# Attention with pooled keys and a squared-ReLU feed-forward: the queries of chunks 2 to 11 are turned one step sooner, and their scores stay where they were

## The chip, the cores and the metric

One core of one Trainium2 chip runs the whole problem. The metric is the device time of the launch in microseconds (us). The core's engines run side by side, each with its own queue of instructions in the order of the program: TensorE (PE, matmuls), VectorE (DVE), ScalarE (ACT), GpSimd (POOL) and SyncE (SP), whose queue issues every DMA. An instruction at the head of a queue that waits holds up all that stand behind it in that queue.

## The reference

Each of 8 batches has 8 heads of 576 tokens with 64 numbers each. Keys and values are averaged over groups of 8 tokens, so each head has 72 pooled keys. A feed-forward net of 512 to 2048 to 512 follows, on the 4608 tokens of all batches.

```python
def _attn_ref(q, k, v):
    k_p = k.reshape(B, H, Sp, 8, D).mean(axis=3)
    v_p = v.reshape(B, H, Sp, 8, D).mean(axis=3)
    scores = (1.0 / np.sqrt(D)) * np.matmul(q, k_p.transpose(0, 1, 3, 2))
    scores = scores - np.max(scores, axis=-1, keepdims=True)
    attn = np.exp(scores)
    attn = attn / (np.sum(attn, axis=-1, keepdims=True) + 1e-09)
    return np.matmul(attn, v_p)

x = attn_out.transpose(0, 2, 1, 3).reshape(B * S, H * D)
h = np.maximum(x @ w_in, 0.0)
out = h * h @ w_out
```

## The kernel before

**Chunks and steps.** The 4608 tokens are cut into 12 chunks of 384. A chunk's feed-forward runs in 16 steps, one for each 128 columns of the hidden layer, so that the program is a row of 192 steps (and two at the end), numbered here `16 c + fc`. Step s emits for PE, in this order: the hidden matmuls of step s (`hidden`, tile `h`), then what attention work for PE is due in that step, then the output matmuls of step s-2 (`project`, tile `o`, LAG is 2). From chunk 1 on each factor is split in a high and a low part, so `hidden` has 12 matmuls and `project` 9. What follows for the other engines stands in this order: the split of step s-1's hidden values (`split_hidden`: ACT writes `gh`, DVE `gl`), then the second halves of the step's attention work on PE (`later`: the copies out of PSUM), then the rest of the attention work in the order in which it was registered, then ReLU (`activate`: ACT writes `r`; DVE squares it from chunk 2 on), and, in a chunk's last step of `project`, the copies of the three output banks by ACT (`store`, tile `ob`) and their DMAs.

**Attention of the next chunk.** While a chunk is in its feed-forward, the next one's attention is computed in four head pairs. Each goes through eight stages, each at a step of its own:

```python
    stages = (transpose_q, scores, exponents, send_sums, fetch_sums, reciprocals, fetch_reciprocals, weigh_values)
        for p in range(NPAIR):
            s = c * NFC + first[p]
            at(s - QL, load_q, c, p)
            for d, f in zip(offsets, stages):
                at(s + d, f, c, p)
```

`transpose_q` turns the queries on PE (four matmuls into the PSUM tile `qps`); its second half splits them into the one tile `st`: two ACT casts and two DVE subtractions. `scores` multiplies `st` with the keys `kl` and `kh` (`sps`), and ACT copies the scores to `sc`; POOL takes the maximum over the 72 keys (`mx`). `exponents` subtracts it (DVE), takes the exponential (ACT), and POOL sums it (`tot`). The sums go through DRAM (`rs`, `rc`), DVE takes reciprocals (`rr`), these go out and come back spread over the partitions (`rd`, `rb`). `weigh_values` multiplies with the pooled values `vp` on PE (`av`), DVE scales by `rb`, and ACT and DVE split the result into `xh` and `xl`, the input of the next chunk's `hidden`.

The steps are written out by hand in `STEADY` (chunks 2 to 11) and `EARLY` (chunk 1): the first tuple has the step at which each pair begins, relative to the chunk's first step, and the second the stages' distances from it. With a pair every four steps, several pairs are under way at a time.

**A chunk's layout.** A chunk of one batch alone (2, 3, 5, 6, 8, 9, 11) and a chunk over two batches (4, 7, 10) write `st` in different strides.

**Keys and values of a new batch** (`kv_steps`, from `KV0` = 31 steps before the chunk that needs them first, which are chunks 3, 4, 6, 7, 9 and 10): six loads of keys, each pooled two steps later on DVE (`kp`: a reduction and a copy), two turns of pooled keys on PE (`transpose_k`, tile `kps`) in the relative steps 5 and 8, each split by ACT and DVE into `kh` and `kl`, and eight pooled values on DVE (`vp`). The first turn needs the keys pooled in relative step 4.

**Buffers.** PSUM has three banks for attention (`ps_a`), two for `h`, and one for each of the three `o`. `st` has one buffer, `sc` two. In steps 14 to 29 the weights are split as well (`split_weights`: an ACT copy `w_i` or `w_o` and a DVE subtraction each).

Of the kernel before, what the change touches and what calls it, by code (L numbers as in the profile page):

```python
# [32 lines left out]
def pooled_attn_relu2_ffn(  # L33
# [43 lines left out]
    PRO, RATE, MARGIN = 5, 2, 1  # L77


    STEADY = ((-22, -18, -14, -10), (0, 1, 3, 4, 5, 6, 7, 8))  # L80
    KV0 = -31
    EARLY = ((-19, -16, -13, -10), (0, 2, 3, 5, 5, 6, 7, 8))

# [185 lines left out]
    def segments(c):  # L269
        t, segs = c * CH, []  # L270
        while t < (c + 1) * CH:
            b = t // S
            n = min((b + 1) * S, (c + 1) * CH) - t
            segs.append((b, t - c * CH, n))
            t += n
        return segs
# [361 lines left out]
    for c in range(1, NCH):  # L638
        first, offsets = EARLY if c == 1 else STEADY
        for b, _, _ in segments(c):  # L640
# [64 lines left out]
```

## Time and profile before

| | |
|---|---|
| median of 3 runs | 981.8 us (981.43 to 993.95) |
| the profiled execution | 978.9 us |
| its span, first to last instruction | 977.2 us |
| mean granted TensorE clock | 0.997 |
| PE busy | 947.3 us (97%) |
| DVE busy | 629.2 us (64%) |
| ACT busy | 425.8 us (44%) |
| POOL busy | 401.2 us (41%) |

The profile's "timeline" has one row for each run of like instructions: start in us, duration in us, engine, operation, output tile and inputs, shapes, the count, and in brackets how long the engine had been idle before and what ended it. SPq is the DMA queue on SP. "Waits" sums such idle times. "Windows" gives the busy time of each engine in a stretch. A pair of rows of a same kind may overlap a little, since an engine begins the next instruction before the last has drained; so the step lengths are better read from one start to the next.

### The profile page before, as it was taken

The page shows a single profiled execution, that of the slowest core. Times are in us where ns is not written, and L with a number is a line of the kernel's source. Part 1 is how long each engine was busy: PE and PEld are TensorE (multiplying, and loading weights), DVE is VectorE, ACT ScalarE, POOL GpSimd, SP SyncE. Part 2 cuts the span into 40 slices and gives each one's busy share as a digit, 9 for nine tenths or more (in the row PEclk, how much of TensorE's full clock was granted, in tenths as well). Part 3 has the DMA queues.
Part 4 walks back from the last instruction along what each step waited for, and adds up shares of the span by engine and source line. Part 5 has one row for each costly group of instructions (what it writes and reads, how often), then busy time and mean ns, then how long its engine had stood idle before and what let it go on. Part 6 is the DMA issues. An engine that isn't in the chain of part 4 may idle for free.

```text
span 977.2 us, 13363 instructions
## 1 busy us (share of the span) xinstructions
PE 947.3 (97%) x4888; PEld 785.9 (80%) x4888; DVE 629.2 (64%) x1034; ACT 425.8 (44%) x847; POOL 401.2 (41%) x209
## 2 busy tenths in 40 slices
PE   6889989999999999999999999999999999999998
PEld 5544458878888888888888888888888888888997
DVE  5869997886775555776776554777677455453221
ACT  2745457674334344334434434433443434432322
POOL 4398635463444434343435335343534434340000
PEclk9999999999999999999999999999999999999999
DMA  9944203112211002112112001211221100100000
GB/s 244 354 147 163 82 17 98 49 51 82 60 56 49 25 26 74 57 52 87 49 50 74 19 23 60 66 48 36 98 57 43 58 26 17 58 10 9 33 1 32
DMA packets 53361, 64.45 MB, mean 66 GB/s; under 512 B 14936, under 2 KB 34480, under 8 KB 53296
## 3 DMA queue, kind: packets, MB, share of 16 engines
q1 hardware_dynamic: 53296, 63.61, 20.9%
q8 instruction: 38, 0.62, 0.3%
q14 instruction: 27, 0.22, 0.1%
HBM read 53.87 MB, written 9.71 MB: 65 GB/s over the span
## 4 chain that ended last, share of the span: by engine, by line
PE 77%; DVE 13%; issue 5%; ACT 4%; POOL 0%; DMA 0%; POOLq 0%; DVEq 0%; ACTq 0%; SPq 0%
PE o L29 34%; PE h L29 33%; PE sps L29 3%; PE av L29 3%; DVE wf_o L29 3%; DVE wf_i L29 2%; PE qps L29 2%; DVE st L29 2%; DVE r L29 1%; ACT st L29 1%; DVE vp L29 1%; DVE sc L29 1%; ACT gh L29 1%; DVE rb L29 1%; ACT xh L29 1%
## 5 line engine op out<-in xcount | busy, mean ns | idle before, releaser
L29 PE MATMUL h<-xh,w_i 128*128 128x384 f32 x1408 | 389.0, 337 | 0.0
L29 PE MATMUL o<-w_o,gh 128*128 128x512 f32 x1056 | 333.7, 397 | 0.0
L29 POOL PARTITION_ALL_REDUCE tot<-sc x88 | 250.2, 2890 | 192.5 <-issue 179.3
L29 PEld LDWEIGHTS h<-xh,w_i 128*128 128x128 f32 x1408 | 258.7, 188 | 8.4 <-issue 0.5
L29 POOL PARTITION_ALL_REDUCE mx<-sc x88 | 138.2, 1618 | 268.8 <-ACT sc L29 268.8
L29 PE MATMUL h<-xl,w_i 128*128 128x384 f32 x704 | 237.9, 338 | 0.0
L29 PEld LDWEIGHTS o<-w_o,gh 128*128 128x128 f32 x1056 | 193.4, 189 | 32.8 <-issue 1.2
L29 DVE TENSOR_TENSOR gl<-r,gh 128x384 fp32r<-128x384 f32 x176 | 142.6, 810 | 107.8 <-ACT gh L29 107.0
L29 PE MATMUL o<-w_o,gl 128*128 128x512 f32 x528 | 209.0, 396 | 0.0
L29 DVE TENSOR_TENSOR r<-r 128x384 f32<-128x384 f32 x160 | 101.7, 635 | 113.7 <-ACT r L29 113.2
L29 ACT CAST gh<-r 128x384 fp32r<-128x384 f32 x176 | 90.4, 514 | 179.8 <-DVE r L29 179.3
L29 ACT ACTIVATE r<-h 128x384 f32<-128x384 f32 x192 | 94.0, 490 | 106.3 <-PE h L29 105.5
L29 PEld LDWEIGHTS h<-xl,w_i 128*128 128x128 f32 x704 | 132.1, 188 | 8.2 <-issue 0.7
L29 PEld LDWEIGHTS o<-w_o,gl 128*128 128x128 f32 x528 | 99.1, 188 | 22.2
L29 ACT CAST xh<-rb 128x384 fp32r<-128x384 f32 x44 | 22.6, 513 | 136.6 <-DVE rb L29 136.6
L29 DVE TENSOR_TENSOR st<-qps,st 64x384 fp32r<-64x384 f32 x80 | 60.6, 757 | 32.6 <-ACT st L29 32.1
L29 ACT ACTIVATE sc<-sc 72x384 f32<-72x384 f32 x88 | 43.7, 525 | 74.1 <-DVE sc L29 74.1
L29 ACT CAST st<-qps 64x384 fp32r<-64x384 f32 x80 | 59.0, 738 | 0.5
L29 DVE TENSOR_REDUCE vp<-v 72x64 f32<-72x512 f32 x48 | 51.0, 1064 | 0.4
L29 DVE TENSOR_REDUCE kp<-k 96x64 f32<-96x512 f32 x42 | 44.1, 1049 | 3.7 <-DMA k<-in_k_dram 3.7
L29 DVE TENSOR_TENSOR sc<-sc,mx 72x384 f32<-72x384 f32 x88 | 44.5, 545 | 0.0
L29 DVE TENSOR_TENSOR rb<-av,rb 128x384 f32<-128x384 f32 x44 | 24.4, 555 | 30.1 <-PE av L29 29.9
(82 smaller groups left out, 725.9 us busy)
## 6 DMA issues: line engine op xcount, KB each, us to landing
k<-in_k_dram SPq DMA_DIRECT2D x48, 192.0 KB
out_dram<-ob SPq DMA_DIRECT2D x36, 256.0 KB
rb<-rd SPq DMA_DIRECT2D x88, 96.0 KB
raw_i<-in_moe_w_in_dram SPq DMA_DIRECT2D x16, 512.0 KB
raw_o<-in_moe_w_out_dram SPq DMA_DIRECT2D x16, 512.0 KB
v<-in_v_dram SPq DMA_DIRECT2D x48, 144.0 KB
q<-in_q_dram SPq DMA_DIRECT2D x30, 192.0 KB
q<-in_q_dram SPq DMA_DIRECT2D x32, 96.0 KB
```

Source lines behind the costliest of these rows:

```text
L29: return lambda *a, **k: self.tc.keep_in_program_order(f(*a, **k))
```

## The change

In chunks 2 to 11 every pair begins one step sooner, and each stage behind the first stands one step further from the pair's beginning. So `transpose_q` (and `load_q`, four steps ahead of it) moves up by one step, and `scores`, `exponents`, the sums and `weigh_values` stay in their steps. No instruction is added or taken away.

```diff
-    STEADY = ((-22, -18, -14, -10), (0, 1, 3, 4, 5, 6, 7, 8))
+    STEADY = ((-23, -19, -15, -11), (0, 2, 4, 5, 6, 7, 8, 9))
```

Before, a pair's turn stood in the step of `weigh_values` of the pair two ahead of it, one step behind `exponents` of the pair ahead. Now it stands in the step of those `exponents`.

DVE in steps 69 and 70, which lie in chunk 4's feed-forward, before: `gl_4` belongs to step 68, `sc_2` is the subtraction in `exponents` of chunk 5's pair 2, `kp_0` the third pooling of batch 4's keys, `st_3` the queries of pair 3.

```order
L29 TENSOR_TENSOR gl_4_3697<-r_4_3671,gh_4_3696 128x384
L29 TENSOR_TENSOR sc_2_3619<-sc_2_3619,mx_2_0_3620 72x384
L29 TENSOR_TENSOR sc_2_3619<-sc_2_3619,mx_2_1_3621 72x384
L29 TENSOR_REDUCE kp_0_3628<-k_2_3631 96x64
L29 COPY kp_0_3628<-kp_0_3628 96x64
L29 TENSOR_TENSOR r_5_3715<-r_5_3715 128x384
L29 TENSOR_TENSOR gl_5_3756<-r_5_3715,gh_5_3755 128x384
L29 TENSOR_TENSOR rb_1_3700<-av_1_3731,rb_1_3700 128x384
L29 TENSOR_TENSOR xl_3544<-rb_1_3700,xh_3543 128x384
L29 TENSOR_TENSOR st_3_3762<-qps_3_3734,st_3_3762 64x2x2x96 x2
```

The same place of DVE now:

```order
L29 TENSOR_TENSOR gl_4_3702<-r_4_3671,gh_4_3701 128x384
L29 TENSOR_TENSOR st_3_3705<-qps_3_3687,st_3_3705 64x2x2x96 x2
L29 TENSOR_TENSOR sc_2_3619<-sc_2_3619,mx_2_0_3620 72x384
L29 TENSOR_TENSOR sc_2_3619<-sc_2_3619,mx_2_1_3621 72x384
L29 TENSOR_REDUCE kp_0_3628<-k_2_3631 96x64
L29 COPY kp_0_3628<-kp_0_3628 96x64
L29 TENSOR_TENSOR r_5_3727<-r_5_3727 128x384
L29 TENSOR_TENSOR gl_5_3763<-r_5_3727,gh_5_3762 128x384
L29 TENSOR_TENSOR rb_1_3710<-av_1_3743,rb_1_3710 128x384
L29 TENSOR_TENSOR xl_3556<-rb_1_3710,xh_3555 128x384
```

The two subtractions of `st_3` moved from behind `xl` to ahead of the exponents' subtractions and of the pooling of `kp_0`. On PE the turn of that pooled tile (`kps`) stands in step 70 behind `av`, as before, without the queries' turn between them.

ACT in steps 65 and 66, before: `ob_0` to `ob_2` empty chunk 3's three output banks, `r_1` is step 65's ReLU, `sc_1` the exponential of chunk 5's pair 1.

```order
L29 ACTIVATE r_0_3476<-h_0_3445 128x384
L29 CAST gh_0_3501<-r_0_3476 128x384
L29 ACTIVATE sc_1_3433<-sc_1_3433 72x384 x2
L29 ACTIVATE r_1_3518<-h_1_3479 128x384
L29 COPY ob_0_3521<-o_0_2850 128x512
L29 COPY ob_1_3524<-o_1_2851 128x512
L29 COPY ob_2_3527<-o_2_2852 128x512
L29 CAST gh_1_3565<-r_1_3518 128x384
L29 CAST xh_3543<-rb_0_3505 128x384
L29 CAST st_2_3572<-qps_2_3548 64x2x2x96 x2
```

The same place of ACT now:

```order
L29 CAST st_2_3510<-qps_2_3492 64x2x2x96 x2
L29 ACTIVATE sc_1_3433<-sc_1_3433 72x384 x2
L29 ACTIVATE r_1_3530<-h_1_3479 128x384
L29 COPY ob_0_3533<-o_0_2858 128x512
L29 COPY ob_1_3536<-o_1_2859 128x512
L29 COPY ob_2_3539<-o_2_2860 128x512
L29 CAST gh_1_3572<-r_1_3530 128x384
L29 CAST xh_3555<-rb_0_3515 128x384
```

The casts of `st_2` moved from behind `xh` to ahead of the exponential, of the ReLU and of the output copies. In step 66 PE's first `project` of chunk 4 writes the bank that `ob_0` reads.

## The prediction

> **What bounds the kernel now.** First the page's busy times, then the waits, then windows of one chunk each.
>
> ```profile
> span 977.2 us, 13363 instructions
> PE 947.3 (97%) x4888; PEld 785.9 (80%) x4888; DVE 629.2 (64%) x1034; ACT 425.8 (44%) x847; POOL 401.2 (41%) x209
> ```
>
> ```profile
> PE sps L29 <- DVE st L29: 8.5, 9, 2.3
> ```
>
> ```profile
> 374.70:452.60 77.90, 75.95 (x391) 65.10 (x390) 55.35 (x86) 32.66 (x65) 31.94 (x16) 1.00 0.20 62
> 452.60:528.70 76.10, 75.89 (x400) 65.45 (x399) 55.77 (x87) 32.07 (x66) 31.94 (x16) 1.00 0.21 64
> 528.70:604.00 75.30, 75.30 (x410) 66.11 (x409) 39.40 (x65) 31.54 (x63) 31.34 (x16) 1.00 0.10 33
> ```
>
> The span is PE's own work; DVE, ACT and POOL have a third of the time or more free. In the waits (total, times, longest) PE's scores have stood 8.5 us for `st`, in nine waits. The windows are the feed-forwards of chunks 4, 5 and 6 (length, then PE busy): almost all PE, with the longest loss where a new batch's values are pooled. So time changes only where PE is made to wait, or stops waiting.
>
> One such wait, in step 75, from three engines' timelines (start, duration):
>
> ```profile
> 422.24 0.51 ACT L29 CAST xh<-rb 128x384 fp32r<-128x384 f32 x1 [2.45 <-DVE rb L29]
> 422.66 1.70 ACT L29 CAST st<-qps 64x384 fp32r<-64x384 f32 x2
> ...
> 424.39 1.67 DVE L29 TENSOR_TENSOR st<-qps,st 64x384 fp32r<-64x384 f32 x2 [1.04 <-ACT st L29]
> 426.10 1.06 DVE L29 TENSOR_REDUCE vp<-v 72x64 f32<-72x512 f32 x1
> ...
> 424.43 0.34 PE L29 MATMUL h<-xh,w_i 128*128 128x384 f32 x1
> 426.21 0.37 PE L29 MATMUL sps<-st,kl 128*72 128x384 f32 x1 [1.45 <-DVE st L29]
> ```
>
> The casts of `st` come behind `xh`, DVE's two subtractions start when both casts are done, and PE's scores follow them.
>
> **What the change takes away.** With two steps between turn and scores `st` is ready a step early, so these waits go. The largest is the one in step 15:
>
> ```profile
> 135.55 0.46 PE L29 MATMUL sps<-st,kl 128*72 128x384 f32 x1 [2.29 <-DVE st L29]
> ...
> 136.77 3.90 PE L29 MATMUL o<-wf_i,r 128*128 128x512 f32 x6
> ...
> 136.60:140.00 3.40, 3.40 (x7) 1.54 (x6) 3.37 (x5) 3.37 (x8) 2.56 (x2) 0.63 0.00 0
> ...
> 137.70 1.92 DVE L29 TENSOR_TENSOR w_i<-wf_i,w_i 128x512 fp32r<-128x512 f32 x2
> ```
>
> It costs 2.3 us and, behind it, 3.4 us at a granted clock of 0.63, another (1 - 0.63) x 3.4 = 1.3. But the next hidden matmuls need `w_i`, which DVE ends at 139.6; what DVE gains is the 1 us that it idles for the casts and some contention. I take 2.0 (between 0 and 3.7). The other eight waits are 8.5 - 2.3 = 6.2 us recorded. Starts show more: 426.21 - 424.43 = 1.78 where the next start is otherwise 0.17 later, 1.61 for a recorded 1.45, since the last matmul's drain covers the rest. Eight times 0.16 is 1.3, and the 31 other score starts may each hide up to 0.1. I take 9.2 (6.2 to 10.6). Together 11.2.
>
> **What it adds: the turn alone on PE.** Step lengths, from start to start of the hidden matmuls:
>
> ```profile
> 397.77 0.33 PE L29 MATMUL h<-xh,w_i 128*128 128x384 f32 x1
> 400.76 0.55 PE L29 MATMUL qps<-ident,q 96*128 96x96 f32 x4
> ...
> 403.49 0.33 PE L29 MATMUL h<-xh,w_i 128*128 128x384 f32 x1
> ...
> 412.56 0.33 PE L29 MATMUL h<-xh,w_i 128*128 128x384 f32 x1
> 414.65 0.41 PE L29 MATMUL kps<-ident,kp 96*128 96x96 f32 x3
> ...
> 417.02 0.33 PE L29 MATMUL h<-xh,w_i 128*128 128x384 f32 x1
> ...
> 566.26 0.33 PE L29 MATMUL h<-xh,w_i 128*128 128x384 f32 x1
> 570.44 0.33 PE L29 MATMUL h<-xh,w_i 128*128 128x384 f32 x1
> 575.93 0.34 PE L29 MATMUL h<-xh,w_i 128*128 128x384 f32 x1
> ...
> 875.05 0.33 PE L29 MATMUL h<-xh,w_i 128*128 128x384 f32 x1
> ...
> 880.23 0.34 PE L29 MATMUL h<-xh,w_i 128*128 128x384 f32 x1
> ```
>
> A bare step is 4.18, one with `av` and `qps` 5.49, one with `av`, `qps` and `kps` 5.72, one with `kps` alone 4.46, one with `av` alone 5.18 (from 875.05). So `kps` costs 0.23 behind other small matmuls and 0.28 alone: a place of its own costs 0.05. `qps` costs 0.31 behind `av`, some 0.36 alone. The 40 turns get a place each: 2.0 us (to 4 if it is twice that).
>
> **What it delays.** ACT and DVE meet the casts and subtractions of `st` first in the step, ahead of `exponents`. Rows for the working:
>
> ```profile
> 415.10 0.40 ACT L29 CAST kh<-kps 128x288 fp32r<-128x288 f32 x1 [1.10 <-PE kps L29]
> ...
> 394.10 1.02 DVE L29 TENSOR_TENSOR sc<-sc,mx 72x384 f32<-72x384 f32 x2
> 395.03 1.08 DVE L29 TENSOR_REDUCE kp<-k 96x64 f32<-96x512 f32 x1
> 396.15 0.92 DVE L29 COPY kp<-kp 96x64 f32<-96x64 f32 x1
> ...
> 394.67 0.99 ACT L29 ACTIVATE sc<-sc 72x384 f32<-72x384 f32 x2 [1.09 <-DVE sc L29]
> ...
> 395.36 5.01 POOL L29 PARTITION_ALL_REDUCE tot<-sc  x2 [4.21 <-issue]
> ...
> 416.49 1.00 ACT L29 ACTIVATE sc<-sc 72x384 f32<-72x384 f32 x2 [0.98 <-DVE sc L29]
> 417.39 0.47 ACT L29 ACTIVATE r<-h 128x384 f32<-128x384 f32 x1
> ...
> 417.17 5.01 POOL L29 PARTITION_ALL_REDUCE tot<-sc  x2 [5.59 <-issue]
> ...
> 419.82 1.92 DVE L29 TENSOR_TENSOR gl<-r,gh 128x384 fp32r<-128x384 f32 x1 [0.58 <-ACT gh L29]
> ```
>
> Count from the step's first hidden matmul, in a chunk of one batch. The turn starts at 2.1 as `kps` does (414.65 - 412.56). The cast `kh` came 0.45 behind the start of three turns; four give 2.75. Casts to subtractions 1.73 (422.66 to 424.39), subtractions 1.71 (to 426.10): DVE reaches the exponents at 6.2. Today it is at 394.10 in a step that began at 397.77 - 4.18 = 393.59, at 0.5. All that stands behind them in the step is 5.7 us later, and two things of it are wanted by PE.
>
> *The turn of the new keys.* The copy of `kp` behind the exponents ends today at 397.07, 3.5 into step 69; now at 9.2. PE's turn `kps` of step 70 needs it. Step 69 lasts 4.18 + 0.36, and `kps` stands where `qps` stood, 400.76 - 397.77 = 2.99 into step 70, at 7.55. PE waits 1.65, once for each of the six batches loaded so: 9.9 us. If DVE's first subtraction needed only the first cast (the row of step 75 speaks against it), it would be 0.85 less, 4.8 in all.
>
> The copy takes 0.92 while POOL sums; it ends 1.7 behind the sum's start, before the first of the two reductions (2.5 each) can be done. The Trainium skill, SBUF — State Buffer, "Who interferes with whom", says that of a GpSimd instruction and a two-port VectorE one the second is blocked for the whole of the first. By that rule the copy would end 0.8 later and the six waits would be 4.8 us dearer, with a time of 997; the trace's row disagrees, so I keep 1.65.
>
> *The output banks.* In step 16c+1 ACT empties three banks behind the ReLU, and PE's `project` in the next step starts by writing the first.
>
> ```profile
> L29 ACT COPY ob<-o x36: 569/588/601, 149.6 to 973.4; 128x512 f32<-128x512 f32 x36
> ```
>
> Exponential 0.57 behind its subtraction, at 6.8; ReLU 0.9 behind that, 7.7; the first copy from 8.1 to 8.7. PE wants the bank at 7.55: 1.2 of waiting, in the boundaries where the pair turned is of a one-batch chunk (steps 33, 65, 81, 113, 129, 161): 7.2. In step 17 the casts of weights and a square stand ahead too: 2.0, an estimate. A two-batch chunk's casts and subtractions are shorter:
>
> ```profile
> 500.57 1.00 ACT L29 CAST st<-qps 64x384 fp32r<-64x384 f32 x2
> ...
> 501.61 1.12 DVE L29 TENSOR_TENSOR st<-qps,st 64x384 fp32r<-64x384 f32 x2 [0.35 <-ACT st L29]
> ```
>
> There the copy ends 1.2 earlier, in time. Banks: 9.2 (3 to 11).
>
> *What stays covered.* The step after next reads `gl` at about 13.0 (4.54 + 5.18 + 2.1 + 0.7 + 0.5); `gl` ended in step 74 at 421.74, 4.6 behind the start of `tot` at 417.17; `tot` will start at 7.5 (1.3 behind the subtraction, as at 394.10 and 395.36), so 12.1. The ReLU frees its bank at 8.2, wanted at 9.7. The sums arrive 5.7 later, and their reciprocal stands three steps behind. SP issues the queries' load ahead of the sums instead of behind, and the key and value loads behind the sums wait as long as these; they have two steps. Where pooled values crowd these steps (first pairs of chunks 3, 6 and 9) the cover of `gl` is near nothing: 1.2 in all (0 to 6).
>
> The sum: 9.9 + 9.2 + 2.0 + 1.2 - 11.2 = +11.1. The profiled execution took 978.9; 990.0. The median of the runs is 2.9 above it: 993, and I say **992**.
>
> **Rivals.**
> - *The waits go and nothing takes their place.* If the exponents begin by 4.5 into the step, the copy of `kp` makes its turn and the banks are free: -11.2 + 2.0 + 1 = -8, or 973. For it: DVE idles a third of the time. Against: the turn cannot start before 2.1, and casts and subtractions take 3.4. Chance 0.10.
> - *Only one of the two new waits is real*, the other met by work that PE finds late anyway: about 983. Chance 0.17.
> - *The clock.* After the wait of 2.3 us the clock fell, which cost 1.3; after that of 1.45 the windows say 1.00. If the thirteen new waits tripped it each time: 17 more, 1009. The Trainium skill, TensorE: Matmul & The Clock Gate, Part 1, has the clock halved after an idle window of about 3.4 us, which none of them reaches; the trace's fall after 2.3 disagrees. Chance 0.08.
> - *The cover of `gl` fails throughout*: 28 one-batch pairs, if `exponents` come 1.4 later than worked out, wait 0.4 each, 11 more: 1003. Chance 0.10.
>
> **The numbers.** The forecast, a little slower, has 0.55, with its own range 986 to 999. The range 981 to 1002 takes in the second rival and part of the last and leaves out about 0.2. A measurement tells some 2% from no change, 20 us: faster than 962 has 0.01, slower than 1001 the clock and half of the last rival, 0.13; the rest 0.86.
>
> **What would show it.** PE waiting for `kp` before `kps` six times at 1.6, and for `ob` before `o` six times at 1.2 and once at 2; no wait of `sps` for `st`; step 15's low clock gone; chunk windows longer by some 1.2 + 1.65 less their old waits. Waits of `kps` and `o` under 0.5 would make it wrong to the fast side; new waits of `o` for `gl`, or a lower clock in the chunks, to the slow side.

## The result, and the profile after

The changed kernel takes 991.8 us (median of 4 runs, 988.7 to 993.2), the kernel before 981.6 in runs beside it: a ratio of 1.0108, with a 95% interval of 1.0072 to 1.0145. So it is a little slower, by less than the 2% that a measurement tells without doubt and by more than nothing. All ratios here, and the times of the experiments, leave out executions in a slower state: one of the kernel before (994.0) and two of the eight of the run with the split behind the exponents (987.5 and 1335.8). The changed kernel's profiled execution took 991.3, 12.4 more than that of before.

The page's busy times of the kernel after:

```profile
span 989.6 us, 13322 instructions
PE 949.6 (96%) x4888; PEld 789.2 (80%) x4888; DVE 644.3 (65%) x1034; ACT 422.1 (43%) x847; POOL 399.9 (40%) x209
```

The span grew by 12.4, PE's busy time by 2.3 of them. The rest is PE waiting. PE's waits after (total, times, longest):

```profile
PE o L29 <- ACT ob L29: 9.4, 7, 2.2
PE kps L29 <- DVE kp L29: 7.0, 6, 1.2
PE h L29 <- ACT r L29: 5.9, 6, 2.1
PE h L29 <- DVE wf_i L29: 1.7, 3, 0.7
PE sps L29 <- ACT st L29: 0.8, 2, 0.6
```

The row of the scores waiting for DVE's `st`, 8.5 us before, is gone. (The last row's two waits were there before too, for ACT and ahead of step 0.) In its place stand the output matmuls waiting for their emptied banks, seven times, and the turn of the pooled keys, six times. The hidden matmuls' waits for ACT's `r` were two and 3.3 us before; of the four that are new, two lie in chunk 0, one of 0.27 at step 16 and one of 0.52 at step 28. Windows of the same three chunks as before (length, then PE busy):

```profile
378.50:456.90 78.40, 76.16 (x392) 65.22 (x391) 54.65 (x81) 31.94 (x64) 31.03 (x16) 1.00 0.21 62
456.90:535.50 78.60, 75.99 (x399) 65.59 (x398) 56.60 (x88) 31.90 (x67) 32.88 (x17) 1.00 0.21 62
535.50:610.80 75.30, 75.30 (x410) 66.30 (x409) 43.39 (x68) 31.14 (x64) 31.34 (x16) 1.00 0.11 33
```

Chunk 4 grew by 0.5, chunk 5 by 2.5 and chunk 6 not at all. All stretches of the program, from start to start of the steps' first hidden matmuls, in us (the launch's first hidden matmul is that of step 0):

| steps | before | after | difference |
|---|---|---|---|
| up to step 0 | 40.62 | 41.24 | +0.62 |
| 0 to 14 | 89.89 | 90.00 | +0.10 |
| 15 | 9.58 | 6.29 | -3.30 |
| 16 to 32 | 83.32 | 87.47 | +4.15 |
| 33 to 48 | 76.01 | 78.28 | +2.27 |
| 49 to 64 | 75.30 | 75.24 | -0.06 |
| 65 to 80 | 77.89 | 78.34 | +0.45 |
| 81 to 96 | 76.04 | 78.66 | +2.62 |
| 97 to 112 | 75.30 | 75.24 | -0.06 |
| 113 to 128 | 77.87 | 78.34 | +0.47 |
| 129 to 144 | 76.03 | 80.23 | +4.21 |
| 145 to 160 | 75.30 | 75.24 | -0.06 |
| 161 to 176 | 73.14 | 74.19 | +1.05 |
| 177 to PE's last matmul | 67.03 | 67.03 | 0.00 |

The gain of step 15 is one place. The losses lie in the stretches in whose steps a new batch is loaded (16 to 48, 65 to 96, 113 to 144); the 1.05 in 161 to 176 is the wait for the banks in step 162. The 0.62 ahead of step 0 lies ahead of everything that the change moves, and is the start-up's own variation.

**Where the time comes from.** Steps 69 and 70 of the kernel after, from four engines' timelines (start, duration):

```profile
398.46 0.33 PE L29 MATMUL h<-xh,w_i 128*128 128x384 f32 x1
...
401.09 1.68 ACT L29 CAST st<-qps 64x384 fp32r<-64x384 f32 x2 [1.91 <-PE qps L29]
...
402.80 1.69 DVE L29 TENSOR_TENSOR st<-qps,st 64x384 fp32r<-64x384 f32 x2 [3.03 <-ACT st L29]
404.52 1.02 DVE L29 TENSOR_TENSOR sc<-sc,mx 72x384 f32<-72x384 f32 x2
405.46 1.05 DVE L29 TENSOR_REDUCE kp<-k 96x64 f32<-96x512 f32 x1
406.55 0.96 DVE L29 COPY kp<-kp 96x64 f32<-96x64 f32 x1
...
403.01 0.34 PE L29 MATMUL h<-xh,w_i 128*128 128x384 f32 x1
...
407.56 0.30 PE L29 MATMUL kps<-ident,kp 96*128 96x96 f32 x1 [1.17 <-DVE kp L29]
...
409.81 0.33 PE L29 MATMUL h<-xh,w_i 128*128 128x384 f32 x1
...
405.79 5.01 POOL L29 PARTITION_ALL_REDUCE tot<-sc  x2 [9.05 <-issue]
```

The chain is the one that the prediction walked: casts of `st`, 2.63 into the step; subtractions at 4.34; the exponents' subtraction at 6.06; the pooling of `kp` ends at 407.51, 9.05 into the step. DVE's 3.03 of idleness ahead of the subtractions is the point: it waits at the head of its queue for ACT's casts, and the pooling that PE wants next stands behind. Step 70 lasts 409.81 - 403.01 = 6.80, where `av` and `kps` without a wait make about 5.41. Steps 65 and 66, the same chain at the banks:

```profile
378.52 0.33 PE L29 MATMUL h<-xh,w_i 128*128 128x384 f32 x1
...
385.18 0.99 ACT L29 ACTIVATE sc<-sc 72x384 f32<-72x384 f32 x2 [2.34 <-DVE sc L29]
386.19 0.49 ACT L29 ACTIVATE r<-h 128x384 f32<-128x384 f32 x1
386.58 1.56 ACT L29 COPY ob<-o 128x512 f32<-128x512 f32 x3
...
387.21 0.73 PE L29 MATMUL o<-w_o,gh 128*128 128x512 f32 x2 [1.08 <-ACT ob L29]
```

The exponential, the ReLU and the first copy start 6.66, 7.67 and 8.06 into step 65; PE gets its bank at 8.69.

**A part that the waits don't show.** Two of the bank waits were followed by a halved clock, one as long was not:

```profile
153.20 0.79 PE L29 MATMUL o<-w_o,gh 128*128 128x512 f32 x1 [2.19 <-ACT ob L29]
...
465.92 0.73 PE L29 MATMUL o<-w_o,gh 128*128 128x512 f32 x2 [1.44 <-ACT ob L29]
...
698.16 0.73 PE L29 MATMUL o<-w_o,gh 128*128 128x512 f32 x2 [1.44 <-ACT ob L29]
```

```profile
153.10:156.50 3.40, 3.30 (x8) 2.62 (x9) 1.32 (x3) 2.19 (x6) 2.36 (x1) 0.50 0.60 232
...
699.30:702.60 3.30, 3.30 (x11) 2.84 (x10) 2.47 (x3) 0.79 (x3) 2.51 (x2) 0.50 0.53 203
...
466.00:469.40 3.40, 3.40 (x17) 3.00 (x18) 2.73 (x3) 1.25 (x3) 3.40 (x2) 1.00 0.62 232
```

PE works through 8 and 11 matmuls at a granted clock of 0.50 in the first two windows and through 17 at 1.00 in the third. Step 18 grew by 3.76 over `av` and `project` alone, 2.19 of it the wait; steps 130 and 131 by 3.09, 1.44 of it the wait. So each fall costs some 1.6.

### The profile page after: what moved, and what is told of

It is laid out like the page before. It is cut to its first block, busy times and chain, and to the rows that moved or that the text cites. A ratio compares the mean times of both kernels' runs of the same rounds, so it can differ in the third digit from the quotient of the medians.

```text
span 989.6 us, 13322 instructions
## 1 busy us (share of the span) xinstructions
PE 949.6 (96%) x4888; PEld 789.2 (80%) x4888; DVE 644.3 (65%) x1034; ACT 422.1 (43%) x847; POOL 399.9 (40%) x209
## 4 chain that ended last, share of the span: by engine, by line
PE 76%; DVE 10%; DMA 5%; ACT 5%; issue 3%; SPq 0%; POOL 0%; DVEq 0%; POOLq 0%
PE o L29 36%; PE h L29 34%; DVE st L29 3%; PE sps L29 3%; DVE wf_o L29 2%; PE av L29 2%; ACT st L29 2%; DMA raw_o<-in_moe_w_out_dram 2%; DVE wf_i L29 2%; DVE sc L29 1%; PE qps L29 1%; DMA k<-in_k_dram 1%; DVE kp L29 1%; ACT sc L29 1%; DMA rb<-rd 1%
## 5 line engine op out<-in xcount | busy, mean ns | idle before, releaser
L29 POOL PARTITION_ALL_REDUCE tot<-sc x88 | 254.2, 2936 | 331.0 <-issue 316.5
L29 PE MATMUL o<-w_o,gh 128*128 128x512 f32 x1056 | 339.4, 403 | 9.4 <-ACT ob L29 9.4
L29 DVE TENSOR_TENSOR gl<-r,gh 128x384 fp32r<-128x384 f32 x176 | 152.1, 864 | 100.1 <-ACT gh L29 100.0
L29 POOL PARTITION_ALL_REDUCE mx<-sc x88 | 132.7, 1555 | 144.8 <-ACT sc L29 144.8
L29 DVE TENSOR_TENSOR r<-r 128x384 f32<-128x384 f32 x160 | 107.8, 674 | 86.6 <-ACT r L29 86.1
L29 PE MATMUL av<-sc,vp 72*64 72x384 f32 (+1 forms) x256 | 43.0, 425 | 0.7 <-ACT sc L29 0.7
```

The lines of the kernel that those rows point to most:

```text
L29: return lambda *a, **k: self.tc.keep_in_program_order(f(*a, **k))
```

## The experiments

The theory was: two new waits make it slower, one on DVE's queue (the pooling of `kp` behind the subtractions of `st`) and one on ACT's (the output copies behind the casts of `st` and the exponential), and each can be taken away alone. The rivals: PE finds other late work as soon as one of them goes; the loss lies in the turn's own place; or it lies with the pairs wherever they stand.

**One wait away: the first turn of the new keys a step later.** From the kernel after:

```diff
-    KV_AT = (..., (5, 8), ...)
+    KV_AT = (..., (6, 8), ...)
```

> The changed kernel, with the first turn of a new batch's keys in relative step 6 instead of 5, so that PE asks for the pooled keys a step later. Theory (the split of the turned queries stands ahead of the exponents and of the key pooling in the same step, and PE waits for what is delayed): the six waits of kps for kp, 1.4 us each from step length, go; 991.8 - 8.4 = 983.4 us, the waits of o for ob stay. Rival (PE's time is lost anyway to the fuller DVE and ACT queues of that step, and a wait taken away comes back at the next thing that PE wants from them): 990 to 992, with new waits of sps or o in steps 71, 119 and so on.

It measured 987.4, 1.0067 of before (1.0046 to 1.0089). Its waits:

```profile
PE o L29 <- ACT ob L29: 9.3, 7, 2.2
...
PE kps L29 <- DVE kp L29: 0.8, 4, 0.3
```

The waits of the keys went, those of the banks stayed as they were: the two are independent. But the span is only 4.0 shorter than that of the kernel after, about half of what was expected. Step 70 is 1.62 shorter, and the turn comes back as 0.36 in step 71 (0.25 is its own place there) and as 0.37 in step 73, so that five batches gain 0.9 each and the first 0.5: 4.9 in all and not 8.4. Then a third fall of the clock, behind the bank wait of step 82, took 1.4 back.

**The other wait away: the output copies ahead of the step's other work.** From the kernel after:

```diff
         for f in later:
             f()
+        if store:
+            store()
...
-        for f in (activate, store):
-            if f:
-                f()
+        if activate:
+            activate()
```

> The changed kernel, with the three copies of the output banks put directly behind the step's follow-up work (the split of the queries), ahead of the exponential and the ReLU, where ACT idles while DVE subtracts. Theory: the seven waits of o for ob go (step lengths: four of 1.15, one of 1.5, one of 2.5 with 0.6 in the step behind it, and 3.8 in step 18, the last two with a low clock): 991.8 - 13.2 = 978.6 us, and the waits of kps for kp stay. Rival (the wait comes back elsewhere): 989 to 992.

It measured 982.4, 1.0020 of before (0.9995 to 1.0044). No `o` waits for `ob` any more. The turns of the keys wait as before, and now three of these six waits are followed by a slow stretch. Here is one that is, and one of the same length that is not:

```profile
170.83 0.30 PE L29 MATMUL kps<-ident,kp 96*128 96x96 f32 x1 [1.20 <-DVE kp L29]
...
250.19 0.30 PE L29 MATMUL kps<-ident,kp 96*128 96x96 f32 x1 [1.17 <-DVE kp L29]
```

```profile
171.00:174.40 3.40, 3.40 (x10) 2.63 (x10) 3.29 (x4) 0.99 (x2) 3.35 (x2) 0.50 0.01 3
250.20:253.60 3.40, 3.40 (x17) 3.00 (x18) 2.78 (x3) 0.51 (x1) 3.23 (x2) 1.00 0.00 0
```

In this profiled execution (982.6) that is the difference to the 978.6 that was expected: the steps of the banks are 12.9 shorter, as expected, and steps 22, 70 and 86 are together 4.6 longer, since the clock fell behind waits that had not made it fall in the kernel after. The run's other executions lost less clock (mean 0.995 to 1.000, here 0.993) and took 979.7 to 987.1, so for the median the cause of the difference is not shown.

**Both away**, the two edits above together:

> Both edits in the changed kernel. Theory: 991.8 - 8.4 - 13.2 = 970 us, that is, faster than the kernel before by what its own waits of sps for st cost, less 2 for the turn alone on PE. Rival: near 989.

It measured 974.1, 0.9927 of before (0.9903 to 0.9952). So with both waits gone the change is a gain, and the two waits are all of the loss. The clock stayed at 1.00. It is 4 us less of a gain than expected. The step-by-step difference to the kernel after names the place: the banks gain 12.9, but the keys' turns gain 4.9 and not 8.4, as in the run with their edit alone. Step 70 is 1.62 shorter, the first turn then costs 0.37 in step 71, and step 73 with the second turn is 0.36 longer than in the kernel after. The second turn in the timelines of PE and DVE:

```profile
411.50 0.78 PE L29 MATMUL kps<-ident,kp 96*128 96x96 f32 x3
...
410.69 1.02 DVE L29 TENSOR_REDUCE kp<-k 96x64 f32<-96x512 f32 x1
411.74 0.19 DVE L29 COPY kp<-kp 96x64 f32<-96x64 f32 x1
```

The third of the turn's three matmuls can go only when the copy ends at 411.93; the three take 0.62 from start to start of what follows, where the kernel after takes 0.25. DVE comes to this pooling late because PE, without the wait in step 70, no longer gives it 1.4 us to catch up.

**The same by another way: the split of the turned queries behind the exponents.** From the kernel after, the turn stays in its earlier step, and its casts and subtractions run behind the step's other attention work:

```diff
-        later = [f(*a) for f, a in todo if f in on_pe]
+        later, turned = [], []
+        for f, a in todo:
+            if f in on_pe:
+                (turned if f is transpose_q and a[0] > 1 else later).append(f(*a))
...
+        for f in turned:
+            f()
```

> The changed kernel, with the split of the turned queries (casts on ACT, subtractions on DVE) put behind the step's other attention work, the exponents and the pooling; the turn on PE stays one step sooner. Theory: the delay has one root, the place of the split in the queues, so both kinds of new wait go at once, with neither of the other two edits: about 970 us, no kps wait for kp, no o wait for ob, no sps wait for st. Rival (the loss is the turn's place on PE, or the sum of work in that step): above 980.

It measured 975.6 (969.8 to 976.6), 0.9922 of before (0.9889 to 0.9955). The only one left of all the waits in question is this:

```profile
PE o L29 <- ACT ob L29: 1.0, 1, 1.0
```

So the loss comes neither from where PE turns the queries, nor from their loads (issued as early here as in the kernel after), nor from the turn's own place (still paid here: steps of 4.55 and 5.19 for 4.18 and 5.49), but from where the turn's second half stands in the queues of ACT and DVE. Its profiled execution reached step 0 at 47.3 us, that of before at 40.6, in a part that this edit doesn't touch; from step 0 on it is 9.0 us shorter than before.

**The change for pairs 0 and 1 alone**, and **for pairs 2 and 3 alone**. Pairs 0 and 1 had the old waits; pairs 2 and 3 turn their queries in the steps of the banks and of the pooled keys. From the kernel before:

```diff
-            s = c * NFC + first[p]
+            sooner = c > 1 and p < 2
+            s = c * NFC + first[p] - sooner
...
-                at(s + d, f, c, p)
+                at(s + d + (sooner and f is not transpose_q), f, c, p)
```

> Only pairs 0 and 1 of each chunk have the change, pairs 2 and 3 keep the steps of before. Theory (each new wait belongs to one pair: the keys' first turn stands in the step after pair 3's turn of queries, the copies of the output banks in the step of pair 2's): none of the new waits, and nearly all of the old ones go, since the long ones were those of pairs 0 and 1 (step 15 3.3, steps 27 to 159 8.0 together); 20 turns of a place of their own cost 1.2. From 980 for the kernel before: 970 us. Rival (the split ahead of the exponents costs in every step where it stands): 975 to 985, half of the change's loss.

It measured 978.5, 0.9969 of before (0.9938 to 0.9999), where 970 was expected. None of the new waits is there, but three old ones are:

```profile
PE sps L29 <- DVE st L29: 5.1, 3, 2.0
```

They are pair 2's, in steps 19, 83 and 131, which had next to none before (step 83 took 5.01, where an undisturbed step with scores takes 4.88). The second, in DVE's and PE's timelines:

```profile
452.60 0.34 PE L29 MATMUL h<-xh,w_i 128*128 128x384 f32 x1
...
456.16 1.02 DVE L29 TENSOR_TENSOR sc<-sc,mx 72x384 f32<-72x384 f32 x2
...
464.66 1.68 DVE L29 TENSOR_TENSOR st<-qps,st 64x384 fp32r<-64x384 f32 x2 [1.05 <-ACT st L29]
...
466.48 0.37 PE L29 MATMUL sps<-st,kl 128*72 128x384 f32 x1 [1.93 <-DVE st L29]
```

The same place in the kernel before:

```profile
453.56 1.02 DVE L29 TENSOR_TENSOR sc<-sc,mx 72x384 f32<-72x384 f32 x2
```

Step 81 begins at 452.60 here and at 452.63 there, but DVE gets to the exponents' subtraction 3.56 into it instead of 0.93. The reading is that the waits of steps 75 and 79 had let DVE and ACT catch up with the eight pooled values that crowd these steps. Without them PE goes ahead, and the backlog meets the next pair that has only one step to spare. The sizes fit: these two steps are 2.3 shorter here, and DVE starts the last of the pooled values 0.7 behind the start of step 81, where the kernel before starts it 1.9 ahead. Then the clock fell as well, from 467.4 on, and the step took 8.57 instead of 5.01. A wait taken from one pair is in part handed to the next. From step 0 on the profiled execution is 3.2 shorter than that of before, where 10 was expected, and steps 19, 83 and 131, together 6.8 longer, are the difference. (It reached step 0 at 46.5, 5.9 later than that of before.)

For pairs 2 and 3 the condition is `p > 1`.

> Only pairs 2 and 3 have the change. Theory: all of the new waits (kps for kp 8.4, o for ob 9.9 and 1 to 3 of low clock behind them), 1.2 for the turns, and only 1.8 of the old waits gone: 980 + 19 = 999 us, slower than the whole change. Rival: 985, half of the change's loss.

It measured 1003.4, 1.0223 of before (1.0183 to 1.0263), with old waits and new ones side by side:

```profile
PE sps L29 <- DVE st L29: 9.1, 9, 2.3
...
PE o L29 <- ACT ob L29: 8.6, 7, 2.2
PE kps L29 <- DVE kp L29: 7.1, 6, 1.2
```

So the new waits are all pairs 2 and 3's, and the old ones that the change takes away are pairs 0 and 1's. The two halves do not add up to the whole (-3 and +22 against +10). Part of it is that pair 2's waits in the run with pairs 0 and 1, 6.8 us with the clock, exist only where pair 2 keeps its one step, and so in that half and not in the whole; and the clock fell in other places in each run.

**No step moved at all: the split of the queries ahead of that of the weighed values.** If the old waits come from `st` standing behind `xh` and `xl`, these two can change places within the step. From the kernel before, for chunks 2 to 11:

```diff
-        later = [f(*a) for f, a in todo if f in on_pe]
+        later = [(f is not transpose_q or a[0] < 2, f(*a)) for f, a in todo if f in on_pe]
+        later = [f for _, f in sorted(later, key=lambda x: x[0])]
```

> The kernel before with its own steps; only where the turn of queries and the weighing of values share a step, the split of the queries stands ahead of the scaling of the weighed values in the queues of ACT and DVE. Theory (the old waits of sps for st came from the casts standing behind xh, which waits for rb and so for the low part of the hidden values; the cast can begin 2 us sooner, and st is then ready before its scores): the waits of before go without the turn's place of its own on PE and without the new waits: 980 - 12 = 968 us. Rival (one step between turn and scores is too short whatever the order): 976 to 980, and the waits of sps for st stay, shorter.

It measured 968.6 us (967.0 to 970.9), 0.9872 of before (0.9835 to 0.9909): faster than both kernels. ACT, DVE and PE in steps 74 and 75:

```profile
415.20 1.70 ACT L29 CAST st<-qps 64x384 fp32r<-64x384 f32 x2 [0.79 <-PE qps L29]
...
416.93 1.69 DVE L29 TENSOR_TENSOR st<-qps,st 64x384 fp32r<-64x384 f32 x2 [0.57 <-ACT st L29]
...
419.20 0.34 PE L29 MATMUL sps<-st,kl 128*72 128x384 f32 x1
```

`st` is whole at 418.62, and the scores follow at 419.20 without a wait. No wait for `st` is left, the turn needs no place of its own, the exponents stay where they were, and of the waits that the change brought only one of 0.40 for `kp` appears. From step 0 on it is 12.0 us shorter than before. This is all that the change aimed at, without what it costs.

## Why the prediction was right, point by point

The sum was +11.1, and the profiled execution grew by 12.4. The waits came where they were said to come and in the number that was said; the sizes were off in both directions. That 992 lies 0.2 from the measured median is luck: the errors of the terms below largely cancel, and the 2.9 that I added from the profiled execution to the median was 0.5 in the kernel after. In us:

| step of the sum | predicted | measured | read from |
|---|---|---|---|
| old wait of step 15 | -2.0 | -3.3 | step 15: 9.58 to 6.29 |
| the other waits for `st` | -9.2 | -10.0 | the 39 other steps with scores, now 4.9 each |
| the turn alone | +2.0 | +2.4 | 40 x 0.06 |
| the new keys' turn | +9.9 | +8.4 | 6 x 1.40 |
| the output banks | +9.2 | +12.9 | 4 x 1.14, then 1.52, 3.09 and 3.76 |
| the tail | +1.2 | +1.1 | steps 27, 28, 79, 80, 128 |
| start-up and the rest | - | +0.9 | 0.62 ahead of step 0, and step 16: 4.67 to 4.97 |

**Step 15** was mis-sized because I let `w_i` take back much of what the wait gives. It took back little. The scores start without a wait, and the clock stays up:

```profile
133.53 0.63 PE L29 MATMUL sps<-st,kl 128*72 128x384 f32 x1
...
133.50:137.00 3.50, 3.50 (x12) 1.69 (x10) 2.82 (x6) 2.54 (x5) 0.63 (x1) 1.00 0.02 1
137.00:140.50 3.50, 2.91 (x14) 2.33 (x14) 3.47 (x6) 3.44 (x9) 2.01 (x2) 1.00 0.02 5
...
137.53 0.44 PE L29 MATMUL h<-xh,w_i 128*128 128x384 f32 x1 [0.27 <-ACT r L29]
...
138.47 0.61 PE L29 MATMUL h<-xh,w_i 128*128 128x384 f32 x2 [0.32 <-DVE w_i L29]
```

The next hidden matmul waits 0.27 for ACT's `r`, and the third of them 0.32 for DVE's `w_i`, so that step 16 is 0.30 longer. Of the 3.3 gained in step 15 (2.3 of wait, 1.0 of clock) 3.0 stay, the upper part of my 0 to 3.7.

**The new keys' turn** was 1.65 in the sum and is 1.40. The working had the copy of `kp` end at 9.2; it ended at 9.05. And it had the whole turn at 7.55, while only the third of its matmuls needs that copy. The other reading, that DVE's first subtraction needs only the first cast, falls: DVE starts at 402.80, when both casts (401.09, 1.68) are done. By the rule of the Trainium skill that the prediction weighed (SBUF — State Buffer, "Who interferes with whom") the copy would have ended 0.8 later. The row of the kernel after speaks against it as that of before did: the copy ends at 407.51, 1.72 behind the start of the sums at 405.79, when the first of two reductions in 5.01 us cannot be done. The copy is held up all the same, only not for so long: it takes 0.96 here, and 0.19 in step 73 of the run with both edits, where no sum runs beside it. By these two rows some 0.8 of each wait (an estimate) is POOL's sum of the exponents, which starts just ahead of the copy; the prediction's 0.92 from before had it in.

**The banks** were right where the mechanism was alone: 8.7 for the first copy's end and 8.69 measured, 1.2 predicted and 1.14 measured. The step of the working that failed is "1.2 of waiting, in the boundaries where the pair turned is of a one-batch chunk", six times the same. In steps 82 and 130 the wait is 1.44 instead of 1.08, since DVE and ACT come to these boundaries late: in step 81 the casts of `st` begin at 2.99, in step 65 at 2.63. That this is the backlog of the eight pooled values, as in the run with pairs 0 and 1, is likely and not shown by itself. And some 3 of the 12.9 are the clock's, in steps 18 and 130, for which the sum had nothing; with it the term lies outside its own 3 to 11, without it at 9.7.

**The tail** has the right size by luck. I put it on the cover of `gl`, and no matmul on PE waits for `gl`. Half of the 1.1 is the one wait of 0.52 of step 28's hidden matmuls for ACT's `r`: there it was the ReLU that came too late, which the working had in time by 1.5 (8.2 for 9.7).

**The rivals.** That nothing takes the waits' place, and that only one of the two waits is real, fell in the trace; the runs that took each away alone showed it again. That `gl` loses its cover throughout did not happen: no matmul on PE waits for it, and the undisturbed steps take 4.18, 4.55 and 4.88. The clock is the rival that I priced wrongly in kind. I gave it all thirteen waits or none; two of thirteen did it in this trace, for 3.2 us, and so did three of the waits that were left in each of the two runs with one wait away. It does not need a wait of 2.3 us. That also bears on the page that the prediction cited: the Trainium skill, TensorE: Matmul & The Clock Gate, Part 1, puts the halving behind an idle window of about 3.4 us, and no wait here reaches even three quarters of that. The same part calls the window free-running, which the starts of the slow stretches, below, agree with.

## What to carry to other kernels

Moving a producer earlier moves everything in its second half, and what counts is what that second half then stands ahead of in each in-order queue: walk that queue for every step that it now shares, and name what PE wants from behind it. Before moving a step, look whether the late piece is only behind a neighbour within its own step; here two lines that swap them beat the change by 2.3%. And a bound engine's waits let the others catch up, so a wait taken away may come back in part at the next place with little slack.

## What the runs showed of the hardware

**Short waits can halve PE's clock.** The granted clock fell to 0.50 for 3.4 us behind waits of 2.19 and 1.44 in the kernel after and of 1.20 in the run with the banks first, and not behind others of 1.44 and 1.17. In the traces the slow stretches start on a fixed grid: the two of the kernel after begin at 153.08 and 699.21, 546.13 apart, which is 160 times 3.413; three of the run with the banks first begin at 171.0, 403.1 and 481.6, which lie 68 and 23 times 3.413 apart. In these two kernels the new waits behind which it fell ended within about 1 us ahead of such a boundary (the one to 153.20 was still on when it came), and those that ended about 1.2 or more ahead did not. Other runs break that rule: with pairs 2 and 3 alone, waits of 1.08 (to 475.92) and 1.46 (to 676.83) ended 0.1 and 0.6 ahead of a boundary and the clock stayed, and with the split behind, it fell at 75.66 behind a wait of 2.11 that had ended 1.3 ahead. So the grid is shown; what within it decides stays open, and no run moved a wait against it.

**The start-up varies.** Step 0 began between 40.6 and 47.3 us in the profiled executions, ahead of everything that these edits touch. A few us between two profiles are to be looked for there first; the stretches of the table behind its first row are safe from it.
